# Sparse attention and a top-2 mixture of experts on one Trainium2 core: four experts take their second and third row tiles as plain products

## The chip, the core and the metric

The kernel runs on one core of one Trainium2 chip. The metric is the time of one execution in device microseconds, taken as the median of several runs. Five engines work beside each other, each with a queue that it runs in order: TensorE (PE in the profile; its weight loads are PEld), VectorE (DVE), ScalarE (ACT), GpSimd (POOL) and SyncE (SP), which only issues transfers.

## The reference

The computation has two stages. Stage one is attention over 4 batches, 8 heads, 576 rows and 64 columns, in which every row keeps its 32 highest scores:

```
scores = scale * q @ k.T
kth    = the 32nd highest score of each row
scores = where(scores >= kth, scores, -1e9)
attn   = exp(scores - max);  attn /= sum(attn) + 1e-9
x      = attn @ v                     # [4 * 576, 512] after joining the heads
```

Stage two routes each of the 2304 rows of x to two of eight experts and adds their weighted results:

```
noisy = x @ w_gate + log1p(exp(x @ w_noise)) * noise
top2, gates = the two highest of the eight, softmax over them
for e in range(8):
    rows = the rows that chose e
    out[rows] += gate * (relu(x[rows] @ w1[e]) @ w2[e])      # 512 -> 1024 -> 512
```

Results have to be as accurate as fp32.

## The kernel before

**Attention.** A tile is 128 rows of one head, or the last 64 rows of two heads. Each pair of heads gives 9 tiles, each batch 36, the kernel 144. `attend(j)` makes one tile: PE multiplies queries by keys in two halves (line 590, line 586 in batch 0), ACT moves the first half to memory (line 598), DVE folds the halves into maxima and minima (line 620) and finds the 32nd highest by four rounds of the eight highest and their removal (lines 624 and 629). A mask is made from it on ACT (line 685) or DVE (line 654), POOL, rarely DVE, subtracts it (line 695), and ACT takes the exponential, which also leaves each row's sum (line 650). `finish` transposes the weights on PE (line 718). `gather`, three times for each pair of heads, multiplies them by the values (lines 780 to 792), lifts the result (line 805), transposes it back (line 809), and normalises: DVE adds 1e-9 to the sums (line 815), takes reciprocals (lines 818 and 820) and multiplies as it leaves PSUM (line 828), or ACT does so in several activations (line 832). `gate` and `route` follow after each pair and each batch: they compute the experts' choices and scatter the batch's rows into the experts' lists in memory (line 1071 on POOL).

**Experts.** Each list is read in tiles of 128 rows. `GROUPS` says after which batch which tiles are taken: each entry is a batch, a first row and a number of tiles, for all eight experts. A group of one tile uses plain fp32 products (`up1`, `down1`), straight from the loaded weights. A group of two tiles uses split products (`up`, `down`): weights, rows and hidden values are each split into a high and a low part, and three fast products replace one plain one. An expert's weights come in four parts of 256 hidden columns; one part is called a unit below. In a plain unit `up1` multiplies rows (as weights of the array) by weights (line 1256), ACT applies the relu (line 1260), PE transposes it (line 1266) and ACT copies it (line 1270); `down1` follows (line 1301). In a split unit ACT makes the two high halves of the weights (line 1139), POOL or DVE the two low ones (line 1143), PE runs 24 products of 256 columns (lines 1227 to 1229) and 12 of 512 (lines 1309 to 1311), ACT and DVE split the hidden values (lines 1233 and 1237). A group's rows are loaded (line 1162), transposed (line 1193) and, for split groups, split (lines 1197 and 1200). Results are added to the output by indirect transfers on POOL (line 1329).

**Order.** `Plan.order` sorts all pieces of work by a list schedule with a duration for each piece, a priority (low numbers first; ten per attention tile) and, for some, a second engine that may take the piece. It writes one fixed order for each engine. `PACE` sets where the units of a group stand among the tiles; numbers like `NORM`, `BIAS` and `LOWS` weigh the choice of engine. A piece with `lock` is kept off times at which the other of DVE and POOL runs such a piece.

```
GROUPS = [(0, 0, 1), (2, 128, 2), (3, 384, 2)]
PACE = [(70, 54), (90, 13), (0, -20)]
...
base, step = (10 * (36 * (bl + 1)) + PACE[gi][0], PACE[gi][1]) if not lastg else (10 ** 5, 1)
```

## Time and profile before

| what | value |
|---|---|
| median of 3 runs | 1008.56 us (1004.54 to 1010.16) |
| the profiled execution | 1016.17 us, its span 1014.2 us |
| PE busy | 924.2 us, 91% |
| DVE busy | 727.9 us, 72% |
| POOL busy | 698.9 us, 69% |
| ACT busy | 686.0 us, 68% |
| mean granted PE clock | 0.969 of full |

The time is a little longer than the span, which runs from the first instruction to the last. A busy share is an average over all stages; the stages have to be looked at one by one. Busy times of PE are modelled and count some waiting; how long products really take shows in the distance from one start to the next. Counts in the profile are of instructions of the chip: each plain fp32 product of the program is two of them, and an exponential of line 650 is two (the second reads the sums).

### The profile page before, as it was taken

How to read it: one execution, taken by the hardware profiler on the slowest of the kernel's cores; microseconds unless marked ns; L12 is line 12 of the kernel's file. 1: busy time of each engine (PE TensorE's matmuls, PEld its weight loads, DVE VectorE, ACT ScalarE, POOL GpSimd, SP SyncE). 2: the span in 40 equal slices, each digit the busy share in tenths (PEclk: the TensorE clock that was granted, in tenths of full speed). 3: DMA queues.
4: the chain of work that ended last, by engine and by line, in shares of the span. 5: the costliest groups of instructions: out<-in, count | busy, mean ns of one | idle time of the engine just before them, and what ended most of it. 6: DMA issues, size and time to landing. Idle time of an engine off the chain costs nothing. (4 is left out here: it accounts for less than half of the span.)

```text
span 1014.2 us, 18197 instructions
## 1 busy us (share of the span) xinstructions
PE 924.2 (91%) x5963; PEld 714.2 (70%) x5979; DVE 727.9 (72%) x2311; ACT 686.0 (68%) x1552; POOL 698.9 (69%) x812
## 2 busy tenths in 40 slices
PE   9999999999988799898859979999897999999993
PEld 4555566566766567666638868887776899989992
DVE  7999999989999879999998974698643332222220
ACT  4898897679887478888757747676743655555550
POOL 4555576756555855656776869977875998888881
PEclk9999999999999989999978989999998999999997
DMA  9375422347467574564592547644466787777741
GB/s 275 110 256 204 130 52 56 127 131 214 140 157 213 189 205 128 156 186 130 171 306 64 168 134 200 193 151 130 138 169 221 231 250 236 222 226 233 225 105 25
DMA packets 109384, 173.80 MB, mean 171 GB/s; under 512 B 7648, under 2 KB 60896, under 8 KB 109280
## 3 DMA queue, kind: packets, MB, share of 16 engines
q1 hardware_dynamic: 100576, 152.32, 47.9%
q0 software_dynamic: 8704, 20.22, 9.0%
q8 instruction: 49, 0.80, 0.3%
q14 instruction: 55, 0.45, 0.2%
HBM read 136.24 MB, written 36.27 MB: 170 GB/s over the span
## 5 line engine op out<-in xcount | busy, mean ns | idle before, releaser
L1143 POOL TENSOR_TENSOR wl<-wr,wh 128x1024 fp32r<-128x1024 f32 x105 | 259.2, 2527 | 46.1 <-ACT wh L1139 42.7
L624 DVE MAX8 t8s<-cat 128x8 f32<-128x288 f32 (+3 forms) x576 | 268.7, 490 | 3.4 <-POOL cat L638 1.1
L695 POOL TENSOR_TENSOR ss<-ss,mk 128x576 f32<-128x576 f32 x141 | 185.1, 1321 | 102.4 <-ACT mk L685 87.1
L1139 ACT ACTIVATE wh<-wr 128x1024 fp32r<-128x1024 f32 x128 | 133.2, 1056 | 48.4 <-PE bk L1311 28.9
L629 DVE MATCH_REPLACE8 cat<-t8s,cat 128x208 f32<-128x208 f32 (+2 forms) x415 | 163.3, 396 | 0.0
L1227 PE MATMUL hps<-xh,wh 128*128 128x256 f32 x512 | 150.0, 293 | 8.2 <-DVE hl L1237 8.2
L1229 PE MATMUL hps<-xh,wl 128*128 128x256 f32 x512 | 146.2, 286 | 2.1 <-POOL wl L1143 1.5
L1228 PE MATMUL hps<-xl,wh 128*128 128x256 f32 x512 | 145.4, 284 | 0.0
L650 ACT ACTIVATE ss<-ss,nb 128x576 f32<-128x576 f32 x144 | 112.5, 781 | 47.9 <-POOL ss L695 33.1
L1237 DVE SCALAR_TENSOR_TENSOR hl<-hps,hh 128x256 fp32r<-128x256 f32 x128 | 53.6, 420 | 125.7 <-ACT hh L1233 124.5
L620 DVE TENSOR_TENSOR cat<-bk,ss 128x288 f32<-128x288 f32 x288 | 126.2, 445 | 15.0 <-ACT ss L598 15.0
L598 ACT ACTIVATE ss<-bk 128x288 f32<-128x288 f32 x288 | 109.2, 416 | 36.8 <-PE bk L590 12.1
L590 PE MATMUL bk<-hi 128*128 128x288 f32 x240 | 89.3, 381 | 25.1 <-DVE cat L620 15.5
L685 ACT ACTIVATE mk<-ss,under 128x576 bf16<-128x576 f32 x115 | 89.0, 777 | 26.5 <-POOL under L681 19.2
L1227 PEld LDWEIGHTS hps<-xh,wh 128*128 128x128 f32 x512 | 98.4, 192 | 11.6 <-DVE hl L1237 9.4
L1233 ACT ACTIVATE hh<-hps 128x256 fp32r<-128x256 f32 x128 | 48.5, 380 | 81.6 <-PE hps L1229 56.4
L718 PE MATMUL pp<-ident,ss 128*128 128x128 f32 x576 | 92.2, 284 | 11.8 <-ACT ss L650 6.8
L1229 PEld LDWEIGHTS hps<-xh,wl 128*128 128x128 f32 x512 | 98.2, 192 | 3.0 <-POOL wl L1143 1.9
L1228 PEld LDWEIGHTS hps<-xl,wh 128*128 128x128 f32 x512 | 98.4, 192 | 1.8
L718 PEld LDWEIGHTS pp<-ident,ss 128*128 128x128 f32 x576 | 67.8, 145 | 39.1 <-ACT ss L650 13.8
L727 ACT ACTIVATE pt<-pp 128x512 f32<-128x512 f32 x144 | 86.6, 601 | 9.1 <-PE pp L718 8.2
L1311 PE MATMUL bk<-wh,hl 128*128 128x512 f32 x192 | 76.8, 400 | 8.4 <-DVE hl L1237 8.4
(158 smaller groups left out, 2037.8 us busy)
## 6 DMA issues: line engine op xcount, KB each, us to landing
wr<-in_w_dram SPq DMA_DIRECT2D x192, 512.0 KB
raw<-in_qk_dram SPq DMA_DIRECT2D x48, 320.0 KB
xg<-xs SPq DMA_DIRECT2D x16, 528.0 KB
xs<-xg SPq DMA_DIRECT2D x16, 528.0 KB
vt<-in_v_dram SPq DMA_DIRECT2D x32, 192.0 KB
out_dram<-xs SPq DMA_DIRECT2D x1, 5120.0 KB
hi<-in_qk_dram SPq DMA_DIRECT2D x8, 320.0 KB
xg<-xs SPq DMA_DIRECT2D x8, 264.0 KB
```

The costliest lines, as they stand in the source:

```text
L598: nc.scalar.activation(t["s"][:, c * HS:(c + 1) * HS], t["sp", c], AF.Copy)
L620: nc.vector.tensor_tensor(o, t["sp", 1], t["s"][:, :HS], op=op)
L624: return lambda: nc.vector.max(t["t8"][:, r], t["cat"] if r == 3 else t["cat"][:, slice(*TAKE[r])])
L629: nc.vector.match_replace(g, t["t8"][:, r], g, NEG)
L650: nc.scalar.activation(t["s"], t["s"], AF.Exp, bias=t["nb"], scale=SCALE, accum_out=sums[:, at:at + 1])
L695: ENG[eng].tensor_tensor(t["s"], t["s"], t["mk"], op=OP.subtract)
L718: nc.tensor.transpose(pp[:, c], t["s"][:, k0 + c * 128:k0 + (c + 1) * 128], ident)
L1139: nc.scalar.activation(WS[n][0][:, i], W[n][:, i], AF.Copy)
L1143: return lambda eng: ENG[eng].tensor_tensor(WS[n][1][:, i], W[n][:, i], WS[n][0][:, i].bitcast(F32), op=OP.subtract)
L1227: nc.tensor.matmul(ps[:, :NN], ah, xh, start=(c == 0), stop=False)
L1228: nc.tensor.matmul(ps[:, :NN], ah, xl, start=False, stop=False)
L1229: nc.tensor.matmul(ps[:, :NN], al, xh, start=False, stop=(c == 3))
```

## The change

`GROUPS` gets a fourth entry, the experts. All experts still take tile 0 after batch 0 as plain products, and the last two tiles after batch 3 as split products. Tiles 1 and 2 (rows 128 to 383) were one split group after batch 2. Now experts 0 to 3 keep that; experts 4 to 7 take tile 1 after batch 1 and tile 2 after batch 2, each as a plain group of its own. So 16 of 64 split units become 32 plain ones. `up1` makes the weights the stationary side: eight products of 128 columns give the hidden values already transposed, and the transposes and the second activation go. Normalising moves from each `gather` to once per pair of heads: each gather only copies its result out of PSUM on ACT or DVE (`out_`), then POOL adds 1e-9 to nine columns of sums, DVE takes reciprocals, and POOL or DVE multiplies the pair's columns in memory. The bias of line 645 has POOL as its first engine, `top` loses its lock, and constants that weigh engines and priorities change. A second way of folding is added, but `MINS` is 0 everywhere and it is not used.

```diff
-SIGNS = (10, 10, 7, 5)
+SIGNS = (10, 10, 8, 5)
...
-LOWS = (1700, 1600, 2300)
-LOWN = 25
+LOWS = (2100, 1600, 2300)
+LOWN = 16
...
-GROUPS = [(0, 0, 1), (2, 128, 2), (3, 384, 2)]
+NE2 = 4
-PACE = [(70, 54), (90, 13), (0, -20)]
+GROUPS = [(0, 0, 1, range(8)), (1, 128, 1, range(8 - NE2, 8)), (2, 256, 1, range(8 - NE2, 8)), (2, 128, 2, range(8 - NE2)),
+          (3, 384, 2, range(8))]
+PACE = [(70, 54), (900, 40), (90, 13), (300, 13), (0, 0)]
...
-                x1 = add("DVE", 62, bias, [d], alt=("POOL", 168, BIAS[b]))
+                x1 = add("POOL", 255, bias, [d], alt=("DVE", 115, BIAS[b]))
...
-            nc.vector.tensor_scalar(sums[:, a:a + n], sums[:, a:a + n], 1e-9, None, op0=OP.add)
...
-                nc.vector.tensor_tensor(o, p, r[:, :, :, None].to_broadcast([rows, nq, 2, D]), op=OP.mult)
...
+        q = add("ACT", 51 + 128 * nq / 1.2, out_, [g, AVN["xr", b]], alt=("DVE", 69 + 128 * nq / .96, OUTS[b]), bank=True)
...
+        def plus():
+            nc.gpsimd.tensor_scalar(sums[:, a0:a0 + 9], sums[:, a0:a0 + 9], 1e-9, None, op0=OP.add)
+        def recip():
+            rs = NN["r"] = P["w"].tile([128, 10], F32, name="rs", bufs=2)
+            nc.vector.reciprocal(rs[:, :9], sums[:, a0:a0 + 9])
+            nc.vector.reciprocal(rs[:64, 9:10], sums[64:128, a0 + 8:a0 + 9])
...
+            ENG[eng].tensor_tensor(o, o, r[:, :, :, None].to_broadcast([128, 4, 2, D]), op=OP.mult)
...
+        q = add("POOL", 1480, norm, [r] + done, alt=("DVE", 800, NORM[b]), lock=True)
...
-        x3 = add("DVE", 1000, top, [x2], lock=True)
+        x3 = add("DVE", 1200, top, [x2])
...
-                ps = HN["p", fp] = P["h"].tile([128, 256], F32, name="hps")
-                for c in range(4):
-                    nc.tensor.matmul(ps, X["h", e][:, c, :128], w[:, 0, c * 256:(c + 1) * 256], start=(c == 0), stop=(c == 3))
+                ps = HN["p", fp] = bank()
+                for f in range(2):
+                    for c in range(4):
+                        a = c * 256 + f * 128
+                        nc.tensor.matmul(ps[:, f * 128:(f + 1) * 128], w[:, 0, a:a + 128], X["h", e][:, c, :128], start=(c == 0),
+                                         stop=(c == 3))
...
-                    nc.tensor.transpose(HN["q", fp][:, q], HN["r", fp][:, q], ident)
...
-                nc.scalar.activation(HN["h", fp], HN["q", fp], AF.Copy)
```

Three places in the orders show what moves. Lines of the changed kernel have other numbers: 727 is the subtraction of the mask, 1301 the first plain product, 1328 the second, 606 and 750 the scores and the transposes of attention, 1236 those of an expert's rows.

POOL in the fourth batch, before, near attention tile 123: `wl` is the low half of split weights, `ss` the subtraction that an attention tile waits for.

```order
L1173 CAST tok<-xs 128x2
L1175 COPY gw<-xs 128x2
L1143 TENSOR_TENSOR wl<-wr,wh 128x1024 x2
L695 TENSOR_TENSOR ss<-ss,mk 128x576
L681 TENSOR_SCALAR under<-t8s 128x1
```

The same engine near the same tile, now.

```order
L727 TENSOR_TENSOR ss<-ss,mk 128x576
L1216 CAST tok<-xs 128x1
L1218 COPY gw<-xs 128x1
L870 TENSOR_SCALAR sums<-sums 128x9
L670 TENSOR_SCALAR nb<-t8s 128x1
L1355 MEMSET spacer 1x1
L1356 DMA out_dram<-yo,tok 2560x512
```

No `wl` stands among the first 26 tiles of this batch any more: the first one follows the subtraction of tile 134. The additions of 1e-9 and the biases are there instead.

PE with plain products, before, near tile 79, and now, near tile 114.

```order
L1256 MATMUL hps<-wr,xh 128x256 x4
L1301 MATMUL bk<-wr,hh 128x512 x2
L1266 MATMUL hps<-ident,hl 128x128 x2
L718 MATMUL pp<-ident,ss 128x128 x4
L722 MATMUL bank<-ident,ss 128x128
```

```order
L606 MATMUL bk<-kl,hi 128x288
L1301 MATMUL hps<-xh,wr 128x128 x8
L750 MATMUL pp<-ident,ss 128x128 x4
L1236 MATMUL hps<-ident,xs 128x128 x2
L1328 MATMUL bk<-wr,hh 128x512 x2
```

The transposes of the hidden values are gone, and the first product is eight of 128 columns instead of four of 256. Plain products now stand among the tiles of the fourth batch too. From the transposes of tile 44 to those of tile 106 the order held 116 first plain products and 55 second ones, and holds 272 (of half the columns) and 64. From tile 107 to 115 it held 16 and 9, and holds 56 and 16. From tile 116 to 143 it held 540 first split products and 264 second ones, and holds 168 and 72 of them, with 184 first plain products and 48 second ones. After tile 143 it held 996 and 504 split ones, and holds 984 and 504.

DVE in the third batch, before, near tile 99, and now, near tile 103.

```order
L654 TENSOR_SCALAR mk<-ss,t8s 128x576
L629 MATCH_REPLACE cat<-t8s,cat 128x240
L815 TENSOR_SCALAR sums<-sums 128x4
L820 RECIPROCAL rs<-sums 128x4
L624 MAX t8s<-cat 128x8
```

```order
L636 TENSOR_TENSOR cat<-bk,ss 128x288
L880 TENSOR_TENSOR xr<-xr,rs 128x4x128
L882 TENSOR_TENSOR xr<-xr,rs 64x128
L679 TENSOR_SCALAR mk<-ss,t8s 128x576
L649 MAX t8s<-cat 128x8
```

Additions to the sums have left DVE (48 before), 16 pairs of reciprocals stand for 64 single ones, 27 copies (line 849) for 38 multiplications out of PSUM, and 12 of the 16 new pairs of multiplications in memory (lines 880 and 882) are here, seven of them in the first three batches.

## Rows read from the trace of the kernel before

**Rows 1.** Windows by stage: us, then busy us (count) of PE, PEld, DVE, ACT, POOL; clock; DMA share; GB/s.
```profile
16.40:151.90 135.50, 134.06 (x790) 76.72 (x802) 130.01 (x452) 116.21 (x297) 82.09 (x141) 1.00 0.50 166
151.90:307.30 155.40, 145.51 (x960) 102.29 (x960) 146.68 (x536) 123.69 (x308) 93.85 (x133) 0.99 0.47 134
307.30:474.30 167.00, 146.14 (x942) 107.40 (x941) 153.38 (x513) 125.43 (x329) 105.46 (x171) 0.97 0.60 177
474.30:525.00 50.70, 36.17 (x220) 25.34 (x220) 49.55 (x155) 32.39 (x74) 37.48 (x57) 0.90 0.72 225
525.00:732.00 207.00, 191.41 (x1354) 167.47 (x1355) 159.89 (x446) 141.93 (x301) 158.95 (x128) 0.96 0.52 152
732.00:810.00 78.00, 68.83 (x448) 59.86 (x446) 29.91 (x78) 39.38 (x70) 56.86 (x61) 0.96 0.65 201
810.00:996.00 186.00, 186.00 (x1208) 168.39 (x1207) 49.41 (x101) 100.10 (x168) 155.39 (x100) 1.00 0.69 205
```

**Rows 2.** The same windows for line 650 alone, two instructions for each attention tile.
```profile
474.30:525.00 50.70, 6.90 (x16) 0.90 0.72 225
525.00:732.00 207.00, 23.52 (x55) 0.96 0.52 152
```

**Rows 3.** Groups of PE by line, 525 to 732 us: count | busy us, mean ns | idle before.
```profile
L1227 PE MATMUL hps<-xh,wh 128*128 128x256 f32 x180 | 53.5, 297 | 1.5 <-DVE hl L1237 1.5
...
L1309 PE MATMUL bk<-wh,hh 128*128 128x512 f32 x86 | 35.4, 412 | 0.0
```

**Rows 4.** Timeline of PE: start us, us, line, shape, count; first split products, first and last of 21.
```profile
574.27 0.29 PE L1227 MATMUL hps<-xh,wh 128*128 128x256 f32 x1
...
576.64 0.28 PE L1229 MATMUL hps<-xh,wl 128*128 128x256 f32 x1
```

**Rows 5.** Timeline of PE: second split products, first and last of 6.
```profile
572.10 0.39 PE L1309 MATMUL bk<-wh,hh 128*128 128x512 f32 x1
...
573.25 0.39 PE L1311 MATMUL bk<-wh,hl 128*128 128x512 f32 x1
```

**Rows 6.** Timeline of PE: plain products, a transpose pair, ten 16-column products.
```profile
199.86 1.89 PE L1256 MATMUL hps<-wr,xh 128*128 128x256 f32 x8
...
205.26 1.88 PE L1301 MATMUL bk<-wr,hh 128*128 128x512 f32 x4
...
208.84 0.38 PE L1266 MATMUL hps<-ident,hl 128*128 128x128 f32 x2
...
284.62 1.19 PE L892 MATMUL bank<-wg,pt 128*128 128x16 f32 x10
```

**Rows 7.** Groups of POOL and of ACT by line, 525 to 732 us.
```profile
L1143 POOL TENSOR_TENSOR wl<-wr,wh 128x1024 fp32r<-128x1024 f32 x37 | 90.7, 2509 | 9.3 <-ACT wh L1139 6.3 <-issue 2.0 <-POOL ss L695 0.6
L695 POOL TENSOR_TENSOR ss<-ss,mk 128x576 f32<-128x576 f32 x26 | 34.6, 1332 | 10.4 <-DVE mk L654 8.8 <-ACT mk L685 1.3
...
L1139 ACT ACTIVATE wh<-wr 128x1024 fp32r<-128x1024 f32 x42 | 43.7, 1059 | 11.8 <-PE bk L1311 8.7 <-issue 2.0 <-POOL wl L1143 1.0
```

**Rows 8.** Line 695 on DVE (ns min/median/max, first and last start), and timelines of POOL and PE.
```profile
L695 DVE TENSOR_TENSOR ss<-ss,mk x3: 758/759/7835, 138.0 to 581.9; 128x576 f32<-128x576 f32 x3
...
577.75 5.33 POOL L1143 TENSOR_TENSOR wl<-wr,wh 128x1024 fp32r<-128x1024 f32 x2
...
582.72 5.20 POOL L1143 TENSOR_TENSOR wl<-wr,wh 128x1024 fp32r<-128x1024 f32 x2
...
590.82 0.79 PE L1311 MATMUL bk<-wh,hl 128*128 128x512 f32 x1 [6.15 <-DVE hl L1237]
```

**Rows 9.** Groups of DVE by line, whole run.
```profile
L815 DVE TENSOR_SCALAR sums<-sums 128x4 f32<-128x4 f32 (+1 forms) x48 | 20.8, 434 | 15.3 <-ACT ss L650 15.1
L828 DVE TENSOR_TENSOR xr<-bank,rs 128x256 f32<-128x256 f32 (+1 forms) x38 | 14.5, 382 | 10.6 <-PE bank L809 9.6 <-ACT ss L598 0.4 <-PE bank L722 0.3
L820 DVE RECIPROCAL rs<-sums 128x4 f32<-128x4 f32 x32 | 5.7, 178 | 1.1
L818 DVE RECIPROCAL rs<-sums 64x1 f32<-64x1 f32 x32 | 5.0, 157 | 1.1 <-issue 0.2
```

More of the change, by code (lines that the diff above doesn't have):

```diff
@@ L65 @@
 GLAG = 1
[L67 removed]
+WHEN = (16, 13, -21, -20)
 NB3 = 108
@@ L467, in sparse_attention_moe @@
     nc.gpsimd.iota(C["iota8"], pattern=[[1, 8]], base=0, channel_multiplier=0, allow_small_or_imprecise_dtypes=True)
-    for nm, at in [("first", 0), ("cap", CAP)] + [(("end", g[0]), g[1] + 128 * g[2]) for g in GROUPS[:-1]]:
-        C[nm] = cp.tile([128, 8], F32, name=nm if isinstance(nm, str) else f"end{nm[1]}")
-        nc.gpsimd.iota(C[nm], pattern=[[STRIDE, 8]], base=at, channel_multiplier=0, allow_small_or_imprecise_dtypes=True)
+    ends = {"first": {}, "cap": dict.fromkeys(range(E), CAP)}
+    for b, lo, nt, es in GROUPS[:-1]:
+        for e in es:
+            ends.setdefault(("end", b), {})[e] = lo + 128 * nt
+    for nm, at in ends.items():
+        C[nm] = cp.tile([128, 8], F32, name=nm if isinstance(nm, str) else f"end{nm[1]}")
+        e = 0
+        while e < E:
+            n = next((k for k in range(e, E) if at.get(k, 0) != at.get(e, 0)), E) - e
+            nc.gpsimd.iota(C[nm][:, e:e + n], pattern=[[STRIDE, n]], base=e * STRIDE + at.get(e, 0), channel_multiplier=0,
+                           allow_small_or_imprecise_dtypes=True)
+            e += n
     zc = P["m"].tile([128, 2, XW], F32, name="xs", bufs=1)
@@ L616, in fn @@
             def fn():
-                if op == OP.max:
+                if op == OP.max and "cat" not in t:
                     t["cat"] = W.tile([128, S], F32, name="cat", bufs=NCAT)
@@ L621, in fold, with both, other @@
             return fn
+        def both():
+            t["cat"] = W.tile([128, S], F32, name="cat", bufs=NCAT)
+            s = t["s"].bitcast(I32)
+            nc.gpsimd.tensor_tensor(t["cat"].bitcast(I32)[:, HS:], s[:, HS:], s[:, :HS], op=OP.add)
+        def other():
+            c = t["cat"].bitcast(I32)
+            nc.gpsimd.tensor_tensor(c[:, HS:], c[:, HS:], c[:, :HS], op=OP.subtract)
         def top8(r):
@@ L654, in mask @@
             nc.vector.tensor_scalar(t["mk"], t["s"], t["t8"][:, 3, 7:8], FAR, op0=OP.is_lt, op1=OP.mult)
-        d1 = add("DVE", 367, fold(OP.max), sk)
-        bc = pl.take("cat", NCAT, d1)
+        if spread(j % 36, MINS[b]):
+            d0 = add("POOL", 700, both, sk, lock=True, prio=pl.prio - AHEAD)
+            d1 = add("DVE", 367, fold(OP.max), sk + [(d0, True)])
+            bc = pl.take("cat", NCAT, d0)
+            pl.give(pl_s, d1)
+            d3 = add("POOL", 700, other, [d0, d1], lock=True, prio=pl.prio - AHEAD)
+        else:
+            d1 = add("DVE", 367, fold(OP.max), sk)
+            bc = pl.take("cat", NCAT, d1)
+            d3 = add("DVE", 367, fold(OP.min), sk + [(d1, True)])
+            pl.give(pl_s, d3)
         b8 = t["b8"] = pl.take("t8", NT8, d1)
-        d3 = add("DVE", 367, fold(OP.min), sk + [(d1, True)])
-        pl.give(pl_s, d3)
         d, n2 = d1, None
@@ L674, in attend @@
             else:
-                d = add("DVE", 130 + n / .96, drop8(r), [d])
+                d = add("DVE", 130 + n / .96, drop8(r), [d, d3] if r == 0 and d3.eng == "POOL" else [d])
         d = add("DVE", 670, top8(3), [d, d3])
@@ L1124, in wload @@
         def wload(n):
[L1125 removed]
+            k, fp = divmod(n, 4)
+            e = items[k]
+            m = 4 * e + fp
             def fn():
[L1128 removed]
+                wr = W[m] = P["wr"].tile([128, 2, 1024], F32, name="wr", bufs=NWR)
                 nc.sync.dma_start(wr[:, 0].rearrange("p (c f) -> p c f", c=4),
@@ L1153, in wload @@
             hs.append(add("ACT", 947, sh(1), [a, hs[0]]))
-            ls = [add("POOL", 2360, sl(i), [hs[i]], alt=("DVE", 1140, LOWS[2 if gi == 2 else n >= LOWN]), lock=True) for i in range(2)]
+            ls = [add("POOL", 2360, sl(i), [hs[i]], alt=("DVE", 1140, LOWS[2 if lastg else n >= LOWN]), lock=True) for i in range(2)]
             pl.give(pw, *ls)
@@ L1374, in experts @@
                     down(*pend)
-                    if f == 0 and n + 1 < 4 * E and n > 0:
+                    if f == 0 and n + 1 < 4 * NI and n > 0:
                         wn[n + 1] = wload(n + 1)
@@ L1378, in experts @@
                     pl.give(xd[e][4], un[0])
-                if ff >= 4 and e + 1 < E:
-                    xturn(e + 1, ff - 4)
+                if ff >= 4 and more:
+                    xturn(e1, ff - 4)
                 pend = (e, ff, un, wn[n], xd[e][3])
```

134 lines of the change are left out of this document (60 added, 74 removed).

## The prediction

> **What bounds the kernel now.** I read the busy times by stage first, then PE's products in the timeline, then the groups by line, and last the waits of DVE.
>
> The stages are cut at the exponentials of attention tiles. Up to 474 us the first three batches run; 8 tiles of the fourth end before 525 us and 28 after [rows 2]. In the first three batches DVE is the bound: it is busy 130.0 of 135.5, 146.7 of 155.4 and 153.4 of 167.0 us [rows 1]. PE also looks busy there, but its busy time counts waiting. From 474 to 525 us DVE is again busy 49.6 of 50.7 us. From 525 to 732 us no engine is full: PE 191.4, DVE 159.9, POOL 159.0, ACT 141.9 of 207 us, and PE's granted clock is 0.96 of full. Attention ends at 732 us. What is left of the split group after batch 2 and then the last group follow: 78 us with PE busy 68.8, and 186 us with PE busy all the time at full clock [rows 1].
>
> The stage from 525 to 732 us is the one that the change reshapes. PE runs split products there [rows 3] between attention tiles; POOL makes their low weights, 37 times 2.51 us = 90.7 us, beside 26 subtractions that attention tiles wait for, and ACT makes the high weights, 43.7 us [rows 7]. How these three meet is seen best at 582 us [rows 8]: POOL runs four `wl` in a row from 577.75 to 587.9 us, the subtraction that DVE took over for one tile lasts 7.84 us where the other two took 0.76, and PE then starts a product after 6.15 us of idling for DVE's line 1237, which stood behind that subtraction.
>
> The Trainium skill's page "SBUF — State Buffer", section "Who interferes with whom", says that a DVE instruction with two inputs in SBUF and a GpSimd instruction that reads SBUF exclude each other for a whole instruction. By that rule the row of 7.84 us is a subtraction kept out by `wl` after `wl`; the trace agrees in that it ends after POOL's row of them.
>
> **The price of a product.** 21 first split products start within 2.37 us, 0.119 us apart [rows 4]; six second ones within 1.15 us, 0.23 us apart [rows 5]. A split unit of 24 and 12 is 24 x 0.119 + 12 x 0.23 = 5.6 us for two row tiles. A plain unit took 1.89 us for eight instructions of 256 columns and 1.88 us for four of 512, and 0.38 us for its pair of transposes [rows 6]: 4.15 us for one tile, each figure with the tail of its last product, so a little high. Now the first product is 16 instructions of 128 columns. No row shows it. Half of a 256-column one is 0.118 us; ten products of 16 columns, each with its own load of 128 x 128 fp32 weights, take 1.19 us [rows 6], 0.119 us each, so the loads do not need more. I take 16 x 0.119 = 1.9 us: the unit keeps its product time and loses 0.38 us, 3.78 us in all. The bounds are 3.4 us (no tails) and 5.6 us (loads not hidden at all).
>
> So 16 split units (90 us) become 32 plain ones (121 us), and the other 32 plain units save 12 us: **PE has 19 us more to do.** The change can only pay by where that work lies and by what the other engines no longer do.
>
> **The change part by part**, against the profiled execution.
>
> *First three batches, to 474 us.* DVE's work on normalising was 20.8 + 14.5 + 5.7 + 5.0 = 46 us in the whole run, and it idled 15.3 us before the additions of 1e-9 [rows 9]. It is now 16 pairs of reciprocals (0.178 + 0.157 us each, 5.4 us), 27 copies of at most 0.38 us (10.3), and 12 pairs of multiplications, which I price at 0.76 us by DVE's 576-column subtraction [rows 8] plus 0.38: 13.7 us. That is 29.4 us, 16.6 less, of which three quarters, 12.5 us, lie in the batches that DVE bounds. The idling can at best fall by two thirds with the number of waits, 7.6 us here; POOL now makes the addition and DVE waits for it, so I count none of it. PE gets more plain work among these tiles: 116 first and 55 second products were 116 x 0.47 + 55 x 0.94 = 106 us with 58 pairs of transposes at 0.38 (22 us, less if overlapped); 272 and 64 are 272 x 0.238 + 64 x 0.94 = 125 us. With the transposes at half of that row, PE has 8 us more. In PE's queue attention's scores stand behind products of up to 1.9 us. I let half of it through: 12.5 - 4, about **-8 us**; bounds -20 and +13.
>
> *474 to 525 us.* PE's plain work rises from 16 x 0.47 + 9 x 0.94 = 16 to 56 x 0.238 + 16 x 0.94 = 28 us, 12 us more, and PE is idle for 14.5 us there [rows 1] under a DVE that is full. **0 us**; bounds -3 and +12.
>
> *525 to 732 us.* Before, 540 and 258 products by the counts of [rows 3] were 64 + 59 = 123 us. Now 168 and 72 split ones are 20 + 17 us, 184 and 48 plain ones 44 + 45 us: 126 us. PE's work stays the same, 3 us more. What can go is the loss: 15.6 us of idling and about 8 us at the lower clock (0.96), 24 us. For it speaks that POOL's 37 `wl` fall to 14 at most (7 split units), all in the last ten tiles, that ACT's 42 high halves fall likewise, and that two thirds of DVE's work for line 1237 (one for each 12 first products) go, so the tiles' own chain through DVE, ACT and POOL runs shorter. I take back 20 of the 24, nearer the full amount because three of the four engines lose work: **-17 us**; bounds +3 and -21.
>
> *After 732 us.* 984 and 504 products are left instead of 996 and 504: 12 x 0.119, **-1 us**. The last route waits for the last normalising, some 1 to 2 us more (a copy, POOL's addition, two reciprocals, a multiplication); the remaining split units of the earlier group cover it, as they cover the route now. Without that cover it costs those 2 us. If the 9 us of idling there [rows 1] went too, -10.
>
> *Priced at nothing.* ACT loses 32 high halves of 1.06 us [rows 7] and gains copies of results; it is busy 142 of 207 us at most [rows 1] and never the bound. SP issues 16 more pairs of weight loads, 1 MB a pair, and four more row loads, ahead of keys and queries in its queue. A plain unit reads 1 MB in 3.8 us, 276 GB/s; the transfers made 152 GB/s at a share of 0.52 from 525 us [rows 1], so 290 GB/s would fill them. Spread among tiles this fits; back to back it would just be covered, and with a late load the unit waits, not the tile.
>
> **Sum.** -8 + 0 - 17 - 1 = -26 us. The profiled execution took 1016.2 us, 7.6 above the median of the runs, so 990 us there and, taken off the median of 1008.6, **983 us**.
>
> **The rivals.**
>
> *All losses go.* Everything in the first three batches (-20), all 24 us after 525 us (-21 net) and 10 of the tail: 1008.6 - 52 = 957 us. For it: no engine is full after 525 us. Against: the same PE order is in place, and routes still hold POOL. Chance 0.14.
>
> *The stalls only move.* DVE waits for POOL's addition and for PE's longer blocks as it did for `wl`, the loss of 24 us stays: -8 to 0, +3, -1: 1003 to 1011, about 1007 us. For it: PE's work after 525 us is the same, and that stage was already 92% busy by PE. Chance 0.10.
>
> *The multiplications are kept out.* They now have both inputs in memory, where the old one read PSUM. If each of the 14 that DVE has in the first three batches waits for one whole subtraction on POOL, 1.33 us [rows 7], that is 19 us on the bounding engine, -26 becomes -7: 1002 us. For it: the row of 7.84 us. Against: the two other such rows took 0.76. Chance 0.06. The skill's rule on the shared pair, on the page named above, asks for such waits, and against the change it says that an operation with one input in PSUM has none.
>
> *Slower: PE's queue.* The plain products among the tiles of the first three batches and of the next stage are 8 + 12 us more; if DVE's idling there is already waiting for scores behind them, all 20 us come through, DVE's saving turns into idling, and the later stage gives +3: 1008.6 + 22, about 1030 us. It decides from the point at which DVE, which idles 22 us between 152 and 474 us now, idles 30 us there: then the 8 us that it saves in those two batches are gone. For it: 19 us more of PE work in total. Against: PE is idle for 31 us between 152 and 474 us in spite of a busy time that counts waiting [rows 1]. Chance 0.08.
>
> That the groups do not stand where they should is no rival: the order holds every plain product before tile 143.
>
> **How the numbers follow.** The forecast has 0.62, with its own range of 966 to 998 us. A measurement can tell about 0.5%, 5 us, from no change. Forecast, first and third rival are faster by more: 0.82; the second is within: 0.10; the fourth is slower: 0.08. The range that holds 8 in 10 reaches from the first rival to the second: 953 to 1006 us; outside lie the fourth, parts of the second and what beats the first.
>
> **What would show it.** Right: the fourth batch takes some 20 us less, with 14 or fewer `wl` on POOL in it and a PE clock near full; the reciprocals and multiplications of lines 874 to 882 on DVE sum to about 19 us; the 16 instructions of a first product start 0.12 us apart; the last group takes 186 us as before. Wrong: batches 2 and 3 last longer than 155 and 167 us with DVE idling before line 636; multiplications of several us on DVE; plain products that wait for weights.

## The result, and the profile after

The changed kernel takes 991.27 us (median of 4 runs, 990.42 to 992.51) where the kernel before took 1007.15 us beside it: a ratio of 0.984, 95% interval 0.981 to 0.988. Run again on another chip (below) it had 986.41 us against 1006.81 us, 0.980 (0.978 to 0.981). So the change is worth 16 to 20 us; the forecast was 26. Sign and range hold; the size was overestimated.

The stages of the changed kernel, cut at the same tiles as [rows 1] (us, then busy us and count of PE, PEld, DVE, ACT, POOL; clock; DMA share; GB/s):

```profile
15.80:152.00 136.20, 135.18 (x797) 77.14 (x806) 128.29 (x442) 116.44 (x290) 84.16 (x142) 1.00 0.49 164
152.00:310.00 158.00, 148.89 (x1088) 110.12 (x1093) 149.28 (x531) 122.12 (x303) 96.89 (x139) 0.99 0.52 150
310.00:475.50 165.50, 149.66 (x1100) 115.92 (x1098) 151.59 (x500) 124.47 (x316) 107.88 (x171) 0.97 0.67 199
475.50:529.00 53.50, 46.27 (x304) 34.13 (x304) 46.88 (x152) 30.33 (x77) 36.70 (x63) 0.97 0.72 221
529.00:712.40 183.40, 177.44 (x1248) 139.97 (x1247) 120.91 (x357) 112.23 (x272) 103.56 (x118) 1.00 0.75 231
712.40:785.00 72.60, 67.51 (x450) 58.91 (x449) 27.64 (x77) 37.92 (x70) 57.24 (x60) 0.98 0.66 207
785.00:970.70 185.70, 185.70 (x1200) 167.99 (x1199) 49.50 (x101) 101.19 (x168) 155.03 (x100) 1.00 0.69 205
```

Against [rows 1] nearly all of the gain lies in one stage: tiles 116 to 143 take 183.4 us instead of 207.0. The tiles before them gain nothing. In that stage PE is now busy 177.4 of 183.4 us at full clock, and the groups of POOL and ACT there, which answer to [rows 7], have shrunk:

```profile
L727 POOL TENSOR_TENSOR ss<-ss,mk 128x576 f32<-128x576 f32 x27 | 37.2, 1379 | 15.0 <-DVE mk L679 8.3 <-ACT mk L717 4.1 <-PE bk L1328 2.3
L1186 POOL TENSOR_TENSOR wl<-wr,wh 128x1024 fp32r<-128x1024 f32 x12 | 29.2, 2494 | 6.0 <-ACT wh L1182 5.2 <-POOL under L713 0.7
L1182 ACT ACTIVATE wh<-wr 128x1024 fp32r<-128x1024 f32 x14 | 14.5, 1055 | 5.6 <-issue 2.8 <-PE bk L1338 2.8
```

POOL's low halves fell from 37 to 12 (90.7 to 29.2 us), ACT's high halves from 42 to 14.

The new first product, in the line's own view (ns min/median/max) and in PE's timeline, with a second product behind it:

```profile
L1301 PE MATMUL hps<-xh,wr x256: 270/275/377, 206.2 to 319.3; 128*128 128x128 f32 x128
...
206.23 1.95 PE L1301 MATMUL hps<-xh,wr 128*128 128x128 f32 x16
...
210.84 1.88 PE L1328 MATMUL bk<-wr,hh 128*128 128x512 f32 x4
```

Sixteen instructions of 0.275 us end within 1.95 us, so they start (1.95 - 0.275) / 15 = 0.112 us apart. The forecast took 0.119; the loads do not show.

The normalising on DVE, whole run, answers to [rows 9]; below it, the multiplications of line 880 in the line's own view (ns min/median/max):

```profile
L849 DVE COPY xr<-bank 128x256 f32<-128x256 f32 (+1 forms) x27 | 9.6, 355 | 26.9 <-PE bank L841 24.5 <-PE bank L754 0.9 <-ACT pt L925 0.9
L880 DVE TENSOR_TENSOR xr<-xr,rs 128x512 f32<-128x512 f32 x12 | 8.8, 733 | 0.0
L874 DVE RECIPROCAL rs<-sums 128x9 f32<-128x9 f32 x16 | 3.4, 213 | 15.7 <-POOL sums L870 15.3
L882 DVE TENSOR_TENSOR xr<-xr,rs 64x128 f32<-64x128 f32 x12 | 3.3, 276 | 0.0
...
L875 DVE RECIPROCAL rs<-sums 64x1 f32<-64x1 f32 x16 | 2.5, 158 | 0.2
...
L880 DVE TENSOR_TENSOR xr<-xr,rs x12: 664/680/1345, 212.1 to 721.7; 128x512 f32<-128x512 f32 x12
```

Together 27.6 us where it was 46 (forecast 29.4), and reciprocals with multiplications 18.0 (forecast 19). The wait only moved: 15.1 us before the additions then, 15.3 us before the reciprocals now, for POOL's addition. The multiplications were not kept out: most took 0.68 us.

### The profile page after: what moved, and what is told of

The parts are those of the page before. It is cut to its first block, busy times and chain, and to the rows that moved or that the text cites. A ratio compares the mean times of both kernels' runs of the same rounds, so it can differ in the third digit from the quotient of the medians.

```text
span 988.6 us, 18573 instructions
## 1 busy us (share of the span) xinstructions
PE 926.3 (94%) x6229; PEld 711.0 (72%) x6246; DVE 683.0 (69%) x2191; ACT 651.5 (66%) x1502; POOL 650.5 (66%) x819
## 4 chain that ended last, share of the span: by engine, by line
PE 59%; DVE 17%; ACT 8%; POOL 6%; issue 4%; DMA 2%; another core or an unknown queue 1%; SPq 0%; POOLq 0%; DVEq 0%; ACTq 0%
PE hps L1301 6%; DVE t8s L649 6%; PE bk L1328 6%; PE bk L602 5%; DVE cat L654 4%; PE hps L564 4%; PE hps L1270 4%; PE hps L1272 4%; PE hps L1271 4%; PE pp L750 4%; PE bank L812 3%; DVE cat L636 3%; PE bk L606 3%; PE bk L1336 2%; PE bk L1337 2%
## 5 line engine op out<-in xcount | busy, mean ns | idle before, releaser
L1186 POOL TENSOR_TENSOR wl<-wr,wh 128x1024 fp32r<-128x1024 f32 x79 | 194.6, 2529 | 35.8 <-ACT wh L1182 29.5
L614 ACT ACTIVATE ss<-bk 128x288 f32<-128x288 f32 x288 | 111.5, 416 | 39.6 <-PE bk L606 15.1
L1328 PE MATMUL bk<-wr,hh 128*128 128x512 f32 x256 | 127.8, 595 | 0.0
L1301 PE MATMUL hps<-xh,wr 128*128 128x128 f32 x1024 | 127.5, 279 | 0.0
L1301 PEld LDWEIGHTS hps<-xh,wr 128*128 128x128 f32 x1024 | 123.1, 195 | 5.2 <-issue 4.0
L1182 ACT ACTIVATE wh<-wr 128x1024 fp32r<-128x1024 f32 x96 | 99.8, 1055 | 34.8 <-PE bk L1338 17.1
L1270 PE MATMUL hps<-xh,wh 128*128 128x256 f32 x384 | 111.3, 290 | 0.2
L1272 PE MATMUL hps<-xh,wl 128*128 128x256 f32 x384 | 108.8, 283 | 0.4 <-POOL wl L1186 0.4
L1271 PE MATMUL hps<-xl,wh 128*128 128x256 f32 x384 | 108.6, 283 | 0.0
L759 ACT ACTIVATE pt<-pp 128x512 f32<-128x512 f32 x144 | 86.8, 603 | 15.3 <-PE pp L750 14.3
L1356 POOL DMA_INDIRECT out_dram<-yo,tok x40 | 65.1, 1627 | 38.1 <-ACT yo L1352 29.8
L564 PE MATMUL hps<-dummy 128*128 128x512 bf16 x283 | 80.0, 395 | 2.4 <-DVE dummy L458 0.9
## 6 DMA issues: line engine op xcount, KB each, us to landing
wr<-in_w_dram SPq DMA_DIRECT2D x224, 512.0 KB
```

Source lines behind the costliest of these rows:

```text
L564: nc.tensor.matmul(ps, C["dummy"].to_broadcast([128, 128]), C["dummy"].to_broadcast([128, 512]), start=True, stop=True)
L1186: return lambda eng: ENG[eng].tensor_tensor(WS[m][1][:, i], W[m][:, i], WS[m][0][:, i].bitcast(F32), op=OP.subtract)
L1270: nc.tensor.matmul(ps[:, :NN], ah, xh, start=(c == 0), stop=False)
L1271: nc.tensor.matmul(ps[:, :NN], ah, xl, start=False, stop=False)
L1272: nc.tensor.matmul(ps[:, :NN], al, xh, start=False, stop=(c == 3))
L1301: nc.tensor.matmul(ps[:, f * 128:(f + 1) * 128], w[:, 0, a:a + 128], X["h", e][:, c, :128], start=(c == 0), stop=(c == 3))
```

## The experiments

The kernels of a set ran on one chip, and each set on another; the kernel before had a median of 1006.83, 999.86 and 1006.81 us in the three sets. So each time is given as a ratio to the kernel before on its own chip. A ratio does not take out all of the chip. On that of the second set ACT lacks some pauses (last section); the kernel before is 7 us faster there, but the order that the changed kernel has up to tile 108 arrives 7 to 16 us earlier (462.6 and 464.5 us, against 471.5 to 478.6 in the third set and in the profile after). Ratios of the second set for such kernels therefore look better than they would on the other chips. Where sets are compared, the time from tile 116 to the end of the profiled execution is given as well.

**First set: which part of the change pays.**

*The kernel before, once more.*

> The kernel before, unchanged, once more with a profile, because its profiled execution of 1016 us lies 9 us above the median of its runs, while that of the change lies at its median. If those 9 us are an accident of one execution, this one takes 1004 to 1010 us, and the stage of attention tiles 116 to 143, 207 us in the first profile, takes some 198 us (the row of 7.8 us on VectorE is then missing or short). If the profile costs the kernel 9 us every time, it is 1014 to 1018 us again with the same stages.

It took 1008.5 us, with a span of 1006.4 instead of 1014.2. So some 8 us of the first profiled execution were its own: 4 before tile 108 and 5 after attention, where ACT had a pause of 5.9 us at 775 us that this execution lacks. Against the expectation the stage of tiles 116 to 143 took 208.2 us, and one subtraction on DVE again 7.83 us.

*The old normalising in the changed kernel.*

```diff
...
-            ENG[eng].tensor_tensor(o, o, r[:, :, :, None].to_broadcast([128, 4, 2, D]), op=OP.mult)
...
+                nc.vector.tensor_tensor(o, p, r[:, :, :, None].to_broadcast([rows, nq, 2, D]), op=OP.mult)
...
```

> The changed kernel with the old normalising in each gather (additions and reciprocals for each gather, multiplication out of PSUM). Theory 1 (the new groups make the gain; the normalising gave VectorE's time back as other work): 989 to 995 us. Theory 2 (the normalising makes a good part of the gain): 998 us or more, with the fourth batch starting 5 us or more later than 475 us.

995.84 us, ratio 0.987 (0.984 to 0.990). Beside the changed kernel's 0.984 and 0.980 the new normalising is worth 3 to 7 us; the intervals overlap for the first and do not settle the size. Whatever it is worth, it does not lie in the first three batches: with the old normalising tile 108 begins at 473.2 us, where the changed kernel has 475.5 and 478.6. One pause of ACT, of 5.5 us, is missing in this execution; even with it tile 108 would come at about 478.7 us (an estimate), 0 to 3 us later. Theory 2 asked for 480 us or more.

*The old first product in the changed kernel.*

```diff
...
-                        nc.tensor.matmul(ps[:, f * 128:(f + 1) * 128], w[:, 0, a:a + 128], X["h", e][:, c, :128], start=(c == 0),
-                                         stop=(c == 3))
+                    nc.tensor.matmul(ps, X["h", e][:, c, :128], w[:, 0, c * 256:(c + 1) * 256], start=(c == 0), stop=(c == 3))
...
+                    nc.tensor.transpose(HN["q", fp][:, q], HN["r", fp][:, q], ident)
...
```

> The changed kernel with the old first plain product (rows stationary, 256 columns, then a pair of transposes and a second activation in each of 64 plain units, instead of 32 before). The pairs are at most 64 x 0.38 = 24 us of TensorE. Theory 1: 994 to 1002 us, the loss mostly where TensorE is full, from tile 116 on. Rival (the transposes hide in idle time): 990 to 993 us.

1058.12 us, ratio 1.050 (1.047 to 1.053): slower than both kernels, and expected by no theory. Its stages from tile 116 on, to the end of attention and from there to the end of the plain products, and a piece of its timeline:

```profile
526.20:636.20 110.00, 101.36 (x690) 75.03 (x689) 101.99 (x322) 85.73 (x225) 64.20 (x89) 1.00 0.52 161
636.20:745.50 109.30, 96.47 (x402) 61.55 (x401) 6.67 (x40) 28.35 (x82) 25.67 (x56) 1.00 0.83 268
```

```profile
693.32 1.89 PE L1299 MATMUL hps<-wr,xh 128*128 128x256 f32 x8
...
695.25 0.38 ACT L1303 ACTIVATE hl<-hps 128x256 f32<-128x256 f32 x1 [2.31 <-PE hps L1299]
695.91 0.38 PE L1309 MATMUL hps<-ident,hl 128*128 128x128 f32 x2
...
696.74 0.38 ACT L1313 ACTIVATE hh<-hps 128x256 f32<-128x256 f32 x1
697.17 1.12 PE L1344 MATMUL bk<-wr,hh 128*128 128x512 f32 x2 [0.88 <-ACT hh L1313]
698.13 1.89 PE L1299 MATMUL hps<-wr,xh 128*128 128x256 f32 x8
```

The planner put 22.5 of the plain units (180 instructions of eight each) behind attention, where DVE is idle. There a unit takes 4.8 us (693.32 to 698.13) for one row tile: product, ACT, transposes, ACT again, second product. All of the split group's units wait behind them. So the new product matters not by the 0.38 us of its transposes; with it the plain units have one ACT step instead of two, and the planner finds room for them among the tiles. That the shorter chain is what made the room is inferred from the two orders. The edit also puts the first products into the two `hps` buffers, which other pieces of work use; whether the planner lacked room for that reason was not tested.

*The old groups in the changed kernel.*

```diff
-GROUPS = [(0, 0, 1, range(8)), (1, 128, 1, range(8 - NE2, 8)), (2, 256, 1, range(8 - NE2, 8)), (2, 128, 2, range(8 - NE2)),
-          (3, 384, 2, range(8))]
+GROUPS = [(0, 0, 1, range(8)), (2, 128, 2, range(8)), (3, 384, 2, range(8))]
...
-PACE = [(70, 54), (900, 40), (90, 13), (300, 13), (0, 0)]
+PACE = [(70, 54), (90, 13), (0, 0)]
```

> The changed kernel with the groups and the pace of the kernel before (tiles 1 and 2 of all eight experts as one split group after batch 2); new normalising, new first product and the new constants stay. Theory 1: 1000 to 1008 us, within 7 us of the kernel before. Theory 2: 995 us or less. The start of the fourth batch also tells whether the plain products of experts 4 to 7 among the tiles of the third batch ate the gain that was forecast there: 465 to 470 us if so, 473 to 476 us if not.

1010.86 us, ratio 1.004 (1.002 to 1.005). Product, normalising and planner's weights give nothing without the groups. Tile 108 began at 472.7 us, next to the 473 to 476 us named for plain products that did not eat the gain forecast for the first three batches. The stage of tiles 116 to 143 took 211.3 us. No subtraction of a mask lasted over 1.05 us on DVE here, but the stall of [rows 8] is there all the same, on another line. Line 541 is DVE's low half of queries, also a subtraction with two inputs in memory (ns min/median/max; then a row each of POOL's and PE's timeline):

```profile
L541 DVE TENSOR_TENSOR hi<-raw,hi x6: 822/854/8804, 180.5 to 609.5; 64x640 fp32r<-64x640 f32 x6
...
612.78 4.88 POOL L1183 TENSOR_TENSOR wl<-wr,wh 128x1024 fp32r<-128x1024 f32 x2
...
618.86 0.80 PE L1335 MATMUL bk<-wh,hl 128*128 128x512 f32 x1 [5.92 <-DVE hl L1277]
```

It took 8.80 us, from 609.54 us, while POOL went from one operation to the next, two `wl` last; PE then idled 5.92 us for DVE's line 1277 behind it. So this run does not tell what the stage would be without the stall.

**Second set: what made the stage of tiles 116 to 143 long, and how many experts should move.**

*The kernel before without the work of its low halves.*

```diff
-                return lambda eng: ENG[eng].tensor_tensor(WS[n][1][:, i], W[n][:, i], WS[n][0][:, i].bitcast(F32), op=OP.subtract)
+                z = slice(0, 1024 if lastg else 1); return lambda eng: ENG[eng].tensor_tensor(WS[n][1][:, i, z], W[n][:, i, z], WS[n][0][:, i, z].bitcast(F32), op=OP.subtract)
...
-                wh, wl = WS[4 * e + ff // 2]
+                wh, wl = WS[4 * e + ff // 2] if lastg else WS[4 * e + ff // 2][:1] * 2
```

> The kernel before, order of the instructions unchanged, but each low half of the weights of its middle group is worked out for one column instead of 1024 (on POOL and on DVE), and the products that used it take the high half again; the output is therefore not the reference's. PE, ACT and the transfers have the same work as before. Theory A, the forecast's step (c) (POOL's 37 low halves of 2.4 us delay the attention's maskings and so PE): the stage from tile 116 to tile 143 falls from 206-208 us to 185-195 us and the whole to 984-996 us. Rival B (PE and ACT's work of the split units make the stage long by themselves, in a chain product, high half, low half on DVE, second product): the stage stays at 202-208 us and the whole at 1001-1008 us.

977.01 us, ratio 0.977 (0.975 to 0.979). The stage falls as theory A had it, to 189.3 us; the whole lies below theory A's 984 us, on a chip on which the kernel before takes 7 us less. The stages from tile 108 on, cut as [rows 1], of the kernel before (its second execution) and of this one:

```profile
470.30:521.20 50.90, 36.17 (x220) 25.31 (x219) 49.72 (x156) 32.39 (x74) 37.45 (x57) 0.92 0.71 224
521.20:729.40 208.20, 191.11 (x1354) 166.01 (x1355) 159.49 (x446) 141.37 (x301) 158.83 (x128) 0.96 0.52 151
729.40:802.50 73.10, 67.65 (x447) 59.14 (x446) 29.49 (x77) 38.29 (x69) 57.83 (x61) 0.98 0.71 214
```

```profile
465.00:514.20 49.20, 36.05 (x221) 25.37 (x220) 45.67 (x155) 32.50 (x74) 35.97 (x57) 0.91 0.70 219
514.20:703.50 189.30, 185.17 (x1353) 163.31 (x1354) 140.12 (x445) 140.99 (x301) 75.72 (x129) 0.99 0.58 170
703.50:771.40 67.90, 65.50 (x448) 57.95 (x448) 20.98 (x79) 39.05 (x71) 30.44 (x61) 1.00 0.76 236
```

PE and ACT do the same work. POOL's falls from 158.8 to 75.7 us, the stage by 18.9 us and the next by 5.2; the clock rises from 0.96 to 0.99 and PE idles 4.1 us instead of 17.1. The low halves, 37 on POOL and four on DVE in this stage, were the loss.

How they cost it can be followed, since both kernels have one order. These are exponentials of tiles 124 to 126, of the kernel before (second execution), and of tiles 124 and 126 of this one:

```profile
562.88 0.78 ACT L650 ACTIVATE ss<-ss,nb 128x576 f32<-128x576 f32 x1 [0.61 <-POOL ss L695]
584.99 0.78 ACT L650 ACTIVATE ss<-ss,nb 128x576 f32<-128x576 f32 x1 [7.11 <-DVE ss L695]
595.24 0.77 ACT L650 ACTIVATE ss<-ss,nb 128x576 f32<-128x576 f32 x1
```

```profile
555.70 0.78 ACT L650 ACTIVATE ss<-ss,nb 128x576 f32<-128x576 f32 x1 [0.85 <-POOL ss L695]
578.27 0.77 ACT L650 ACTIVATE ss<-ss,nb 128x576 f32<-128x576 f32 x1
```

The same work takes 32.4 us in the one and 22.6 in the other: 9.8 of the 18.9 us lie in these two tiles. They hold the stall of [rows 8]. DVE's subtraction takes 7.83 us before and 0.75 here; before, PE idles 6.2 us for line 1237 behind it and then runs at a granted clock of 0.50, the lower level of 1.2 GHz, from 581.8 to 592.0 us. The other 9 us come in small steps from tile 133 on; PE's direct waits for `wl` are 3.2 us of them. How much of the rest is maskings that stand behind `wl` in POOL's queue, this run does not separate.

*Two experts, and six, in plain groups instead of four.*

```diff
-NE2 = 4
+NE2 = 2
```

> The changed kernel with two experts in plain groups for their second and third tiles instead of four; the four tiles of the other six stay in split products, and by the order 5 split units stand before the exponential of tile 134 again and the rest before the attention's end. Theory A (what gains is that low halves leave POOL while attention runs): about half of the gain is left, 996-1003 us. Rival B (PE's own time; a plain unit pair with its evictions is no cheaper than the split one it replaces): 986-993 us, since PE has some 10 us less to do.

> The changed kernel with six experts in plain groups instead of four. Theory A: PE was 177 us of 183 us busy in the stage of the last tiles, so nothing is left to be gained there; the two further experts put their PE time in excess of the split products (about 4.8 us an expert) onto the path: 995-1003 us. Rival B (the gain grows with each expert moved, as attention's last tiles are freed of more low halves): 978-988 us.

987.66 us, ratio 0.988 (0.986 to 0.990), and 987.82 us, 0.988 (0.986 to 0.990). With two, 0.988 lies between what the theories named (996 us and more, or 993 us and less, over 1007 are 0.989 and 0.986): some 12 us of the gain are left by this ratio. But the run does not put theory A to the test. By its trace only 13 low halves stand before the attention's end, six of them before tile 134, where the expectation counted on all of them; the changed kernel has 14. What came back is split work behind attention: 400 products of line 1272 there instead of 332, and 326.4 us from the end of attention instead of 276.2. With six, 0.988 is the lower end of theory A (995 over 1007) and above rival B: nothing more is won. Its profiled execution was the slowest of its five, 994.7 us. Its stages from tile 116 to the end of attention, and from there to the last group:

```profile
513.90:621.00 107.10, 106.28 (x815) 83.00 (x814) 100.62 (x323) 84.55 (x218) 65.98 (x93) 1.00 0.65 194
621.00:788.50 167.50, 153.39 (x904) 115.88 (x903) 20.51 (x70) 54.21 (x118) 70.76 (x85) 0.98 0.83 270
```

25 plain units (400 instructions of sixteen each) stand behind attention, from 621 to 739 us, 4.7 us a unit. A split unit of the last group, 32 of them from 783.2 to 988.6 us in the changed kernel, takes 205.4 / 32 = 6.4 us for two row tiles, 3.2 a tile. A plain unit alone costs half as much again for its one tile, in a stretch with a DMA share of 0.83 and 270 GB/s.

*The planner's weights of before in the changed kernel.*

```diff
-BIAS = (500, 500, 500, 500)
+BIAS = (800, 700, 1200, -1100)
...
-                x1 = add("POOL", 255, bias, [d], alt=("DVE", 115, BIAS[b]))
+                x1 = add("DVE", 62, bias, [d], alt=("POOL", 168, BIAS[b]))
```

(and likewise the signs, below, low halves, first weights and the route's top)

> The changed kernel with the planner's weights of the kernel before (signs, bias and its engine, below, low halves, first weights, route's top): groups, new first product and new normalising stay. Theory A (DVE was the bound of the first three batches and the new weights filled what the normalising had freed with other work): tile 108 begins 3-8 us earlier than the 475.5 us of the changed kernel, and the whole falls to 983-988 us. Rival B (the weights matter little, or the plain work in the third and fourth batch costs there what it costs): tile 108 at 473-478 us and the whole 989-996 us.

985.62 us, ratio 0.986 (0.985 to 0.988), by the ratio no better than the changed kernel, which was not run on this chip. Its first three batches, and those of the run with two experts, which has the changed kernel's order up to there:

```profile
16.00:148.50 132.50, 130.29 (x772) 75.56 (x784) 125.24 (x431) 113.56 (x287) 86.84 (x148) 1.00 0.50 169
148.50:303.90 155.40, 147.29 (x1069) 106.33 (x1076) 144.42 (x522) 123.75 (x309) 100.33 (x142) 1.00 0.48 143
303.90:462.20 158.30, 144.33 (x1078) 112.83 (x1074) 151.23 (x497) 120.85 (x309) 110.22 (x174) 0.98 0.67 194
```

```profile
16.20:152.30 136.10, 134.68 (x795) 76.85 (x804) 127.70 (x439) 116.37 (x290) 83.97 (x142) 1.00 0.49 164
152.30:304.70 152.40, 147.45 (x1088) 109.19 (x1093) 148.87 (x530) 122.14 (x302) 96.68 (x139) 1.00 0.54 156
304.70:462.60 157.90, 149.37 (x1101) 115.40 (x1099) 151.20 (x502) 124.73 (x315) 107.77 (x171) 0.98 0.71 208
```

DVE has 420.9 us of work in the one and 427.8 in the other, and tile 108 begins at 462.2 and 462.6 us. Seven microseconds less on DVE became seven of idling. Theory A of this run falls: the early tile 108 is the chip's, since the other run has it too. From tile 116 on this kernel takes 470.0 us and the changed one 459.6 and 460.9, so the new weights seem worth some 10 us there.

**Third set: the changed kernel on a chip with pauses, and the best count.**

*The changed kernel, once more.*

> The changed kernel once more, unaltered. Two kernels with the same instructions up to tile 108 reached it at 462.6 and 464.5 us on another chip, where the changed kernel's profile says 475.5 us; its ACT had three pauses ended by something outside of the core's engines (15.7 us in all) that those two lack. Theory A (the late tile 108 was the price of these pauses, which belong to the chip and not to the kernel): where there are no such pauses tile 108 begins at 461-466 us, and the ratio to the kernel before stays at 0.981-0.988. Rival B (the changed kernel's own order is late there): tile 108 at 472-478 us again.

986.41 us, ratio 0.980; the profiled execution was the slowest of its six, 992.9 us. Tile 108 began at 478.6 us, and the pauses were there as well. By itself this neither confirms nor refutes theory A, since this chip has them too. But seven executions have the same instructions up to tile 108, and they sort by ACT's pauses before it: 475.5, 478.6 and 477.1 us (the last without low halves, below) with pauses of 11 to 13 us in all, 471.5 and 472.0 us (three and five experts, below) with the first alone, of 5.5 us, and 462.6 and 464.5 us (second set) with none. That speaks for theory A and against rival B. The stage of tiles 116 to 143 took 183.5 us.

*The changed kernel without the work of the low halves ahead of the last group.*

> The changed kernel with the low halves of the split group ahead of the last one worked out for one column instead of 1024, and its products given the high half again; the output is therefore not the reference's. Theory A (the change has taken the low halves out of the attention's way, and PE is the bound of the last tiles now): 0-8 us less than the changed kernel. Rival B (the 14 low halves that still stand ahead of the attention's end, and those behind it, cost what the 45 cost before): 15-22 us less.

985.02 us, ratio 0.977 (0.974 to 0.979): 3 us less than the changed kernel by the ratios, 1.4 by the medians, with intervals that overlap; theory A. The stage of tiles 116 to 143 takes 179.6 us instead of 183.5. The kernel before without its low halves has the same ratio of 0.977, so most of what the change gains is the low halves; but that was another chip, and from tile 116 on this kernel takes 455.2 us and that one 461.3, so that the rest of the change is worth nothing is not shown.

*Three and five experts.*

> The changed kernel with three experts in plain groups. Theory A (two prices against each other: PE's excess of some 5 us for each expert in plain groups, and low halves in the attention's way, of which four experts already leave few): between the 0.988 of two experts and the 0.984 of four, 0.982-0.988 of the kernel before; a curve flat at its bottom. Rival B (the stall of an odd count, since the split group then begins and ends elsewhere): over 0.990.

> The changed kernel with five experts in plain groups. Theory A: by the same two prices 0.984-0.989, between four experts (0.984) and six (0.988). Rival B (it is the count of split units left for the time behind attention that sets the end, and five leave the fewest without PE waiting): below 0.981, and the best version so far.

996.82 us, 0.991 (0.989 to 0.994), and 994.79 us, 0.987 (0.985 to 0.990).

| experts in plain groups | set | ratio to the kernel before | from tile 116 to the end, us | profiled execution less median, us |
|---|---|---|---|---|
| 0 | first | 1.004 | 485.8 | -2.2 |
| 2 | second | 0.988 | 473.8 | -0.1 |
| 3 | third | 0.991 | 468.9 | -1.8 |
| 4 | result, third | 0.984 and 0.980 | 459.6 and 460.9 | -0.6 and +6.5 |
| 5 | third | 0.987 | 466.1 | -2.8 |
| 6 | second | 0.988 | 478.7 | +6.9 |

Four is the best by either column, and no version with the right output beat the changed kernel. By the ratio three is worse than two, as rival B of that run had it. But two was run on the chip without pauses, where its first 116 tiles took 512.0 us against 524.2; from tile 116 on three is faster than two and slower than four. So a stall of the odd count is not shown, and by these single executions the curve has one bottom, at four or near it (the 466.1 us of five hold a pause of ACT of 5.7 us).

## Why the prediction was right, and where its size was off

| stage | forecast | changed kernel, two executions | kernel before, two executions |
|---|---|---|---|
| to tile 108 | -8 | 475.5, 478.6 | 474.3, 470.3 |
| tiles 108 to 116 | 0 | 53.5, 51.4 | 50.7, 50.9 |
| tiles 116 to 143 | -17 | 183.4, 183.5 | 207.0, 208.2 |
| after attention | -1 | 276.2, 277.4 | 282.2, 277.0 |

The sum came nearer than its terms: what tiles 116 to 143 gave beyond the forecast, some 7 us, made up for a part of what the first three batches did not give. That is luck.

**Tiles 116 to 143: right mechanism, undersized.** The forecast took back 20 of the 24 us of loss because POOL, ACT and DVE lose work, and let 3 us of more PE work through. The stage fell by 23.6 and 24.7 us, beyond the forecast's bound of 21. That the `wl` were the loss is shown twice: without them the kernel before has the stage at 189.3 us, and the changed kernel gains only 1 to 3 us more by losing its own. The term that was too small is PE's: it is busy 177.4 us in the changed kernel, at a clock of 1.00, and 185.2 us in the kernel before without low halves, at 0.99, so there is less PE work in the stage and not 3 us more. PE is the engine nearest to full there now, 177 of 183 us. The stall of 7.8 us that the prediction used as its picture was, with the lower clock behind it, about half of what the low halves cost: 9.8 of 18.9 us.

**The first three batches: the step that failed.** "I let half of it through: 12.5 - 4, about -8 us" rested on "DVE is the bound" there. DVE's normalising up to tile 108 did get cheaper, and the planner gave DVE other work. In the second execution of before and in the profile after, up to tile 108:

```profile
L815 DVE TENSOR_SCALAR sums<-sums 128x4 f32<-128x4 f32 (+1 forms) x36 | 11.5, 320 | 8.3 <-ACT ss L650 8.1
L828 DVE TENSOR_TENSOR xr<-bank,rs 128x256 f32<-128x256 f32 (+1 forms) x26 | 9.9, 382 | 3.2 <-PE bank L809 1.6 <-PE bank L722 0.9 <-ACT ss L598 0.4
L645 DVE TENSOR_SCALAR nb<-t8s 128x1 f32<-128x1 f32 x30 | 6.1, 202 | 0.2
```

```profile
L670 DVE TENSOR_SCALAR nb<-t8s 128x1 f32<-128x1 f32 x46 | 9.2, 199 | 0.1
L849 DVE COPY xr<-bank 128x256 f32<-128x256 f32 (+1 forms) x21 | 7.3, 349 | 4.3 <-PE bank L841 2.0 <-PE bank L754 0.9 <-ACT pt L925 0.9
L880 DVE TENSOR_TENSOR xr<-xr,rs 128x512 f32<-128x512 f32 x7 | 5.4, 772 | 0.0
L874 DVE RECIPROCAL rs<-sums 128x9 f32<-128x9 f32 x12 | 2.6, 213 | 10.2 <-POOL sums L870 9.9
```

Line 645's work, line 670 now, came to DVE 46 times instead of 30. In sum DVE is busy 429.2 us in the three batches (the first three windows of the profile after) where it was 430.1 [rows 1]. The run with the old normalising has tile 108 at 473.2 us: the new one did not bring it forward. The run with the old weights shows the second half of the error: even where DVE really had 7 us less, the tiles came no earlier. A share of 92 to 96% busy did not make DVE the only bound. That the tile's chain through PE, ACT and POOL was as long is the likely reason; it was not shown. On the chip without pauses, the changed kernel's order reached tile 108 at 462.6 us and that of before, which has no low halves up to there, at 465.0: -2 us where -8 was forecast. The rest of the difference in the table goes with ACT's pauses. One sign of being wrong came in half: the second batch took 158.0 us, over 155, but DVE idled only 1.0 us before line 636 in it, and without pauses it took 152.4.

**Tiles 108 to 116** came out near the forecast's 0: +1 to +3 us, and on the chip without pauses 49.4 against 49.2 of the kernel before without its low halves. The 12 us of plain work were covered.

**After attention** the forecast's -1 lies between 0 and -6; the first profiled execution of before, against which the sum was made, had 5 us there, beside a pause of ACT, that its repetition lacks. The last group took 185.7 us in the cut of [rows 1], as before.

**The price of a product** was right: 0.112 us apart against 0.119, so a unit of 1.9 + 1.9 us among the tiles. But the prediction priced a plain unit by PE alone. Behind attention it takes 4.7 us (25 units, six experts), and 4.8 us with the old first product. So the plain work pays only while it fits among the tiles, and the prediction's only word on it ("back to back it would just be covered") was too kind.

**The rivals.** All losses gone (957) did not come: the early tiles gave nothing. The stalls did not merely move: the loss after tile 116 is gone. The multiplications were not kept out. PE's queue (slower) did not decide: on the chip without pauses DVE idled 10.2 us from tile 36 to tile 108 in the changed kernel's order (310.3 us less 148.87 and 151.20) and 15.4 us in that of before (153.6 and 160.6 us less 146.68 and 152.09, the run without low halves); in the profile after it idled 22.6 us there, where the prediction set the mark at 30.

## What to carry to other kernels

An operation on an engine that is not full (POOL, 77% busy in its stage) can still be the loss of that stage, because another engine's instruction is held up beside it or because steps that every tile waits for stand behind it: price it by removing its work and leaving the order, as the run with low halves of one column did, and compare the two kernels at the same instructions to see where the time went. A long row that vanishes in a variant may have come back on another line: look for it before calling it harmless. Work of a higher price on the fullest engine can still pay if it takes such operations away, but only as long as it fits among other work: the same plain units cost half as much again as the split ones once they stand alone. And a planner refills an engine that a change relieves, so a saving there is to be sought in the whole batch's busy time and not in the group of lines that became cheaper.

## What the runs showed of the hardware

A subtraction with two inputs in memory on DVE took many times its usual time while POOL ran operation after operation: 7.83 us beside low halves of 1024 columns, and 0.75 us at the same place of the same order when these had one column; 8.80 us for line 541, where the median is 0.85. It outlasted more than one of POOL's instructions, of 2.5 us each.

ACT had pauses that end with an event from none of the core's engines. In the waits of ACT, the changed kernel and then the kernel before (us in total, times, longest):

```profile
ACT ss L614 <- remote: 8.0, 2, 5.7
ACT hh L1306 <- remote: 7.7, 1, 7.7
```

```profile
ACT hh L1233 <- remote: 5.9, 1, 5.9
ACT ss L598 <- remote: 5.0, 1, 5.0
```

In the changed kernel they end at 191.8, 348.7 and 518.7 us. POOL issued the ten scatters of rows of a route at 177.1 to 188.9, 334.1 to 346.1 and 505.0 to 516.7 us, so each pause ends 2 to 3 us behind the last of ten. Of the eight executions of the changed kernel and its variants outside of the second set, seven have the first one, of 5.5 to 5.7 us. The four kernels of the second set have none; there the changed kernel's order reached tile 108 at 462.6 and 464.5 us instead of 475.5, and the kernel before took 999.86 us instead of 1006.8. The Trainium skill's page "Runtime: NRT & Kernel Launch", section "Instruction fetch mechanics", says that each engine fetches its instructions in blocks of 256 through a DMA queue of its own, and that the cost is mostly hidden. The profile has such queues (51 packets with 0.84 MB on one of them), and a block held up behind the scatters would look like these pauses; that it was one, and why one chip lacks them, was not shown.
